# Slot reads of the first two batches at slots 24 and 29, last two loads of x behind them, and block sums of w_out at slots 13 to 20

## The chip, the core and the metric

The kernel runs on one core of a Trainium2 chip. The metric is the device time of one execution in microseconds (us); the median of ten executions stands for the kernel. A separate profiled execution gives the trace from which all durations below come.

## What is computed

An attention step between a sequence and a small set of state slots is followed by a feed-forward layer with a squared ReLU. The reference, cut to what matters:

```python
B, H, S, Ns, D = 8, 8, 512, 32, 64          # x: B,H,S,D   state: B,H,Ns,D
scale = 1 / sqrt(D)
a     = softmax(scale * x @ state.T)         # over the 32 slots
xread = a @ state                            # B,H,512,64
a2    = softmax(scale * state @ x.T)         # over the 512 positions
sread = a2 @ x                               # B,H,32,64: the "slot read"
X   = concat([xread, sread], axis=2) -> (8*544, 512)
h   = X @ w_in                               # 512 -> 2048
g   = s * relu(h)**2 + b
out = g @ w_out                              # 2048 -> 512, float32
```

## The kernel before

**Slots.** The first 128 of 144 slots belong to the eight batches, 16 to each: slot 16*s + f computes hidden block f (128 of 2048 features) of batch s for its 512 sequence rows. The last 16 slots do the same for the 256 rows of all slot reads. `mm1_x` puts the hidden block into PSUM (two matmuls, tile `h`), ACT applies the ReLU, DVE squares it (`g`). Everything else is attached to slots: `at(slot, fn, ...)` puts a function into a table, and the main loop runs, for each slot, first `mm1_x`, then the functions of that slot in the order in which they were entered, then a share of the second layer's matmuls (tile `o`), taken from `units2`.

**The second layer.** Batch 0 is done plainly in 16 units in slots 11 to 28, into two PSUM banks (`ob`), and evacuated by `mm2_out` (tiles `osb`). Batches 1 to 7 use a scheme with seven block products in place of eight: it needs sums of blocks of g (`pair_sums`, tile `pd`, DVE) and sums of blocks of w_out (`weight_sums(q)`, tile `u`, four DVE instructions for each of the four quarters of w_out). Batch 1's part starts at slot 30.

**Attention of a batch b.** `att_T(b)` makes the scores T from the transposed state and the transposed x; ACT takes the exponential E with its sums. `att_D` and `mm1_x` use E for the sequence side. `att_M` folds the state into w_in (tile `M`). For the slot side, `att_aT(b)` scales E (tile `a`, printed by the profile as `a<-E,q`) and transposes it by two DMA transposes on SP's queue into `aT`; `att_V(b)` multiplies it with x (tile `V`, 32 small matmuls), a DVE copy puts it into `sr`, and one more DMA transpose on SP's queue puts it into `srdT`, which is needed only after slot 128.

**x.** `load_x(b)` is a DMA on POOL's queue that converts to 16 bits on the way; `xn` has six buffers, so batch 6 takes batch 0's buffer and has to wait for `att_V(0)`, and batch 7 waits for `att_V(1)`. For batches 3 to 7 x is transposed by four DMA transposes per batch on SP's queue (`dma_xT`, tile `xT`, two buffers); batches 0 to 2 are transposed on TensorE (`xTps`). The state of batches 3 to 7 is transposed by one DMA, `dma_stT` (tile `stTd`, slot 22).

**Order.** PE, POOL and SP run in the order in which the program writes the instructions; DVE's and ACT's order is made by a scheduler. `aT` has two buffers, so `att_aT(2)` has to wait until `att_V(0)` has read `aT` of batch 0. All of it together, around the change:

```python
    at(21, att_aT, 0)
    at(22, dma_stT)
    for k in range(4):
        at(23 + k, dma_xT, 3, k)
    at(27, att_aT, 1)
    ...
    for b in range(B):
        at(NKF * max(b, 2) + (12 if b != 0 else 8), att_V, b)
```

With NKF = 16 the slot reads of batches 0, 1 and 2 stand at slots 40, 44 and 44, that of batch b from 3 on at slot 16*b + 12. A loop sets `att_T(2)` to slot 22, `att_aT(2)` to slot 27, and `att_T(3)` to slot 32; `dma_xT(4, k)` is entered at slots 28 to 34.

Of the kernel before, what the change touches and what calls it, by code (L numbers as in the profile page):

```python
# [14 lines left out]
def kernel(  # L15
# [13 lines left out]
    nc = tc.nc  # L29
    AF = mybir.ActivationFunctionType  # L30
    ALU = mybir.AluOpType
# [5 lines left out]
    P = 128  # L37
    NKM = DM // P
    NKF = DF // P
# [315 lines left out]
    def at(slot, fn, *args):  # L355
        AT.setdefault(slot, []).append(lambda: fn(*args))
# [14 lines left out]
    at(16, att_stT, 2)  # L371
    at(19, att_xT, 2, 0)
    at(20, att_xT, 2, 1)
    at(21, att_aT, 0)
    at(22, dma_stT)
    for k in range(4):
        at(23 + k, dma_xT, 3, k)
    at(27, att_aT, 1)
    units = []
    for b in range(2, B):  # L380
        units += [(att_T, b)] + [(att_M, b, c) for c in range(4)]
# [1 line left out]
    while i < len(units):  # L383
        for u in units[i : i + 2]:
            at(int(slot), *u)
            if u[0] is att_T:
                b = u[1]
# [6 lines left out]
        i += 2  # L394
        slot += 5.2 if i < 6 else 6.4
    for b in range(B):
        at(NKF * max(b, 2) + (12 if b != 0 else 8), att_V, b)


    G = {}  # L400
# [1 line left out]
    hS = S // 2  # L402
# [18 lines left out]
    def blocks(b, j):  # L421
        return G[b, j].rearrange("p (i k) (h t) -> p i (k h) t", k=2, h=2)

    def pair_sums(b, j):

        g4 = blocks(b, j)
        pd = ppool.tile([P, 2, 4, hS], FP16, name=f"pd_{b}_{j}", tag="pd")
        nc.vector.tensor_tensor(  # L428
            pd[:, :, 0:2],
            g4[:, :, 0:4:3, :],  # L430
            g4[:, :, 1:2, :].to_broadcast((P, 2, 2, hS)),
            ALU.subtract,
        )
        nc.vector.tensor_tensor(pd[:, :, 2], pd[:, :, 0], g4[:, :, 3], ALU.add)  # L434
        nc.vector.tensor_tensor(pd[:, :, 3], g4[:, :, 2], pd[:, :, 2], ALU.subtract)  # L435
        PD[b, j] = pd

# [3 lines left out]
    def wo_blk(q, k, h):  # L441
        return wo[q].rearrange("p (i k) (h n) -> p k h i n", k=2, h=2)[:, k, h]

    def weight_sums(q):
        u = upool.tile([P, 4, 2, hD], FP16, name=f"u_{q}", tag="u")
        held = tc.keep_in_program_order
        held(nc.vector.tensor_tensor(u[:, 0], wo_blk(q, 0, 0), wo_blk(q, 0, 1), ALU.subtract))
        held(nc.vector.tensor_tensor(u[:, 1], wo_blk(q, 1, 1), u[:, 0], ALU.subtract))
        held(
            nc.vector.scalar_tensor_tensor(  # L450
                u[:, 2], wo_blk(q, 0, 1), -1.0, wo_blk(q, 1, 1), ALU.mult, ALU.subtract
            )
        )
        held(nc.vector.tensor_tensor(u[:, 3], wo_blk(q, 1, 0), u[:, 1], ALU.subtract))
        U.append(u)

# [198 lines left out]
    att_M(0, 0)  # L655
    warm_up(2)
    for q in range(4):
        at(20 + 3 * q, weight_sums, q)
    at(41, load_x, 6)
    at(45, load_x, 7)  # L660
    for slot in range(NKF * (B + 1)):
        s, f = divmod(slot, NKF)
        if s < B:
            mm1_x(s, f, s == 0 and f in (7, 8))
        else:
            mm1_sr(f)
        for fn in AT.get(slot, []):
            fn()
        run_units(slot)
        if 0 < s < B and f % 4 == 3:  # L670
            pair_sums(s, f // 4)
# [42 lines left out]
```

## Time and profile before

| what | value |
|---|---|
| median of 10 executions | 226.61 us (226.09 to 229.21) |
| profiled execution, its own time | 228.12 us |
| span in the profile | 226.3 us, so 1.8 us lie around it |
| granted TensorE clock, mean over the span | 0.975 |
| TensorE (PE) busy with matmuls | 209.0 us, 92% of the span |
| VectorE (DVE) busy | 167.6 us, 74% |
| ScalarE (ACT) busy | 131.2 us, 58% |
| DMA | 24.04 MB, mean 106 GB/s |

In the profile, PE is TensorE's matmul and PEld its weight load; a line number such as L67 is often that of a helper (all matmuls are issued by `mm` at L67), so tiles tell more than lines. The slice rows of the page cut the span into 40 equal slices of 5.66 us. In a timeline a row gives the start, the length, the instruction, how many were merged, and in brackets how long the engine had been idle before it and for whom. "q0" is the DMA ring set that POOL's DMAs use, "q1" the one that SP's use.

### The profile page before, as it was taken

The page shows a single profiled execution, that of the slowest core. Times are in us where ns is not written, and L with a number is a line of the kernel's source. Part 1 is how long each engine was busy: PE and PEld are TensorE (multiplying, and loading weights), DVE is VectorE, ACT ScalarE, POOL GpSimd, SP SyncE. Part 2 cuts the span into 40 slices and gives each one's busy share as a digit, 9 for nine tenths or more (in the row PEclk, how much of TensorE's full clock was granted, in tenths as well). Part 3 has the DMA queues.
Part 4 walks back from the last instruction along what each step waited for, and adds up shares of the span by engine and source line. Part 5 has one row for each costly group of instructions (what it writes and reads, how often), then busy time and mean ns, then how long its engine had stood idle before and what let it go on. Part 6 is the DMA issues. An engine that isn't in the chain of part 4 may idle for free.

```text
span 226.3 us, 4920 instructions
## 1 busy us (share of the span) xinstructions
PE 209.0 (92%) x1966; PEld 132.0 (58%) x1966; DVE 167.6 (74%) x394; ACT 131.2 (58%) x287; POOL 34.1 (15%) x56
## 2 busy tenths in 40 slices
PE   7978899997999499999999999999999999999970
PEld 2423343543567247667667667666676776888650
DVE  2478836899999627898798879888987888745330
ACT  3486962398786234885785659749855554432200
POOL 5545002201011301102111110120112102100000
PEclk9999999999999959999999999999999999999996
DMA  7999999999211999343354312312312102111211
GB/s 203 194 198 200 178 192 146 180 234 124 86 49 24 176 177 211 84 91 105 93 127 63 101 47 63 82 52 62 81 46 96 49 6 89 59 46 49 93 25 68
DMA packets 41186, 24.04 MB, mean 106 GB/s; under 512 B 25676, under 2 KB 39244, under 8 KB 41164
## 3 DMA queue, kind: packets, MB, share of 16 engines
q0 software_dynamic: 13744, 15.21, 34.0%
q1 hardware_dynamic: 26860, 8.40, 22.7%
q8 instruction: 15, 0.25, 0.5%
q10 hardware_dynamic: 560, 0.13, 0.3%
q14 instruction: 7, 0.06, 0.1%
HBM read 17.37 MB, written 8.91 MB: 116 GB/s over the span
## 4 chain that ended last, share of the span: by engine, by line
PE 63%; DMA 19%; DVE 13%; POOL 2%; issue 0%; ACT 0%
PE o L67 38%; PE h L67 16%; DMA xn<-in_x_dram 10%; DMA stf<-in_state_dram 4%; DMA aT<-a 3%; PE h_sr L67 3%; DVE g L416 3%; PE Mps L67 3%; DVE pd L428 1%; DVE u L450 1%; PE V L67 1%; DMA ident<-ident_const 1%; DVE c L518 1%; DVE pd L435 1%; DVE M L318 1%; PE D L67 1%
## 5 line engine op out<-in xcount | busy, mean ns | idle before, releaser
L415 ACT ACTIVATE g<-h 128x512 f16<-128x512 f32 x126 | 75.2, 604 | 61.6 <-PE h L67 60.7
L67 PE MATMUL h<-a,M 128*128 128x512 f16 x256 | 76.9, 383 | 0.5 <-DVE a L297 0.3
L416 DVE TENSOR_TENSOR g<-g 128x512 f16<-128x512 f16 x128 | 53.6, 423 | 18.3 <-ACT g L415 17.6
L67 PEld LDWEIGHTS <-pd 128*128 128x128 f16 x448 | 43.2, 98 | 17.5 <-issue 2.7
L67 PEld LDWEIGHTS <-g 128*128 128x128 f16 x400 | 38.1, 99 | 23.2 <-issue 6.5
L67 PE MATMUL o<-wo,g 128*128 128x256 f16 (+1 forms) x288 | 46.8, 297 | 1.9 <-DVE osb L471 1.0
L67 PE MATMUL o<-u,pd 128*128 128x256 f16 x336 | 45.9, 273 | 0.0
L528 POOL DMA_DIRECT2D out_dram<-c x24 | 16.2, 675 | 112.9 <-DVE c L523 92.0
L67 PEld LDWEIGHTS <-M 128*128 128x128 f16 x256 | 24.7, 99 | 9.9 <-issue 1.8
L316 ACT CAST M<-Mps 128x512 f16<-128x512 f32 x46 | 24.9, 604 | 0.5 <-PE Mps L67 0.5
L518 DVE SCALAR_TENSOR_TENSOR c<-o,s_bc,bias_bc 128x512 f32<-128x512 f32 x28 | 20.9, 747 | 2.8 <-PE o L67 2.3
L428 DVE TENSOR_TENSOR pd<-g 128x1024 f16<-128x1024 f16 x28 | 19.3, 688 | 0.6
L67 PE MATMUL o<-u,g 128*128 128x256 f16 x112 | 17.2, 291 | 0.0
L523 DVE SCALAR_TENSOR_TENSOR c<-o,s_bc,c 128x512 f32<-128x512 f32 x21 | 15.7, 746 | 1.6 <-PE o L67 1.6
L318 DVE CAST M<-Mps 128x512 f16<-128x512 f32 x18 | 12.3, 685 | 5.2 <-PE Mps L67 5.2
L67 PE MATMUL o<-wo,pd 128*128 128x256 f16 x112 | 15.7, 273 | 0.0
L415 ACT ACTIVATE g_sr<-h_sr 128x256 f16<-128x256 f32 x16 | 6.1, 383 | 12.1 <-PE h_sr L67 12.1
L280 ACT ACTIVATE E<-T 128x256 f16<-128x256 f32 x32 | 11.9, 399 | 2.0 <-PE T L67 2.0
L435 DVE TENSOR_TENSOR pd<-g,pd 128x512 f16<-128x512 f16 x28 | 11.7, 418 | 0.1
L434 DVE TENSOR_TENSOR pd<-pd,g 128x512 f16<-128x512 f16 x28 | 11.7, 418 | 0.1
L293 ACT ACTIVATE D<-D 128x512 f32<-128x512 f32 x16 | 9.7, 610 | 0.0
L295 ACT ACTIVATE R<-D 128x512 f16<-128x512 f32 x16 | 9.5, 600 | 0.3
(63 smaller groups left out, 156.3 us busy)
## 6 DMA issues: line engine op xcount, KB each, us to landing
out_dram<-c POOLq DMA_DIRECT2D x24, 256.0 KB, 2.6
xn<-in_x_dram POOLq DMA_DIRECT2D x7, 512.0 KB, 23.4
wi<-in_moe_w_in_dram POOLq DMA_DIRECT2D x4, 512.0 KB, 12.0
wo<-in_moe_w_out_dram POOLq DMA_DIRECT2D x4, 512.0 KB, 18.5
xf<-in_x_dram SPq DMA_DIRECT2D x4, 256.0 KB, 3.1
out_dram<-osb POOLq DMA_DIRECT2D x4, 256.0 KB, 9.0
out_dram<-c SPq DMA_DIRECT2D x4, 256.0 KB, 2.5
stf<-in_state_dram SPq DMA_DIRECT2D x1, 320.0 KB, 13.1
```

The costliest lines, as they stand in the source:

```text
L67: return nc.tensor.matmul(out, lhsT, rhs, start=start, stop=stop, tile_position=tp, is_transpose=is_transpose, skip_group_check=True,)
L280: nc.scalar.activation(E[:, 256 * m : 256 * m + 256], T[m][:, g, :], AF.Exp, scale=scale, accum_out=rs[:, g, m : m + 1],)
L316: nc.scalar.copy(dst, ps[g])
L318: nc.vector.tensor_copy(dst, ps[g])
L415: nc.scalar.activation(gt, hps, AF.Relu)
L416: nc.vector.tensor_mul(gt, gt, gt)
L428: nc.vector.tensor_tensor(pd[:, :, 0:2], g4[:, :, 0:4:3, :], g4[:, :, 1:2, :].to_broadcast((P, 2, 2, hS)), ALU.subtract,)
L434: nc.vector.tensor_tensor(pd[:, :, 2], pd[:, :, 0], g4[:, :, 3], ALU.add)
L435: nc.vector.tensor_tensor(pd[:, :, 3], g4[:, :, 2], pd[:, :, 2], ALU.subtract)
L518: nc.vector.scalar_tensor_tensor(t, src, s_bc, add, ALU.mult, ALU.add)
L523: nc.vector.scalar_tensor_tensor(t, src, s_bc, t, ALU.mult, ALU.add)
L528: (nc.sync if b == B - 1 else nc.gpsimd).dma_start(dst[:, rows:SCH:2, hD * h : hD * h + hD], t)
```

## The change

The slot reads of batches 0 and 1 move from slots 40 and 44 to slots 24 and 29. `att_aT(0)` moves from slot 21 to 18, `att_aT(1)` from slot 27 to 19, so that on SP's queue the transposes of batch 1's `a` now stand in front of `stTd` and of the transposes of batch 3's x. `load_x(6)` moves from slot 41 to 25 and `load_x(7)` from slot 45 to 30. The four `weight_sums` move from slots 20, 23, 26, 29 to 13, 15, 17, 20, and signs are turned round in them and in `pair_sums`, so that the third instruction of each is a plain add of two blocks in place of a `scalar_tensor_tensor`; `pair_sums` keeps its three instructions.

```diff
@@ order of the slots
     at(19, att_xT, 2, 0)
     at(20, att_xT, 2, 1)
-    at(21, att_aT, 0)
+    at(18, att_aT, 0)
+    at(19, att_aT, 1)
     at(22, dma_stT)
     for k in range(4):
         at(23 + k, dma_xT, 3, k)
-    at(27, att_aT, 1)
...
     for b in range(B):
-        at(NKF * max(b, 2) + (12 if b != 0 else 8), att_V, b)
+        at((24, 29)[b] if b < 2 else NKF * b + 12, att_V, b)
@@ pair_sums
         nc.vector.tensor_tensor(
             pd[:, :, 0:2],
+            g4[:, :, 1:2, :].to_broadcast((P, 2, 2, hS)),
             g4[:, :, 0:4:3, :],
-            g4[:, :, 1:2, :].to_broadcast((P, 2, 2, hS)),
             ALU.subtract,
         )
-        nc.vector.tensor_tensor(pd[:, :, 2], pd[:, :, 0], g4[:, :, 3], ALU.add)
+        nc.vector.tensor_tensor(pd[:, :, 2], g4[:, :, 3], pd[:, :, 0], ALU.subtract)
         nc.vector.tensor_tensor(pd[:, :, 3], g4[:, :, 2], pd[:, :, 2], ALU.subtract)
@@ weight_sums
-        held(nc.vector.tensor_tensor(u[:, 0], wo_blk(q, 0, 0), wo_blk(q, 0, 1), ALU.subtract))
-        held(nc.vector.tensor_tensor(u[:, 1], wo_blk(q, 1, 1), u[:, 0], ALU.subtract))
-        held(
-            nc.vector.scalar_tensor_tensor(
-                u[:, 2], wo_blk(q, 0, 1), -1.0, wo_blk(q, 1, 1), ALU.mult, ALU.subtract
-            )
-        )
+        held(nc.vector.tensor_tensor(u[:, 0], wo_blk(q, 0, 1), wo_blk(q, 0, 0), ALU.subtract))
+        held(nc.vector.tensor_tensor(u[:, 1], wo_blk(q, 1, 1), u[:, 0], ALU.add))
+        held(nc.vector.tensor_tensor(u[:, 2], wo_blk(q, 0, 1), wo_blk(q, 1, 1), ALU.add))
         held(nc.vector.tensor_tensor(u[:, 3], wo_blk(q, 1, 0), u[:, 1], ALU.subtract))
@@ main loop's table
     for q in range(4):
-        at(20 + 3 * q, weight_sums, q)
-    at(41, load_x, 6)
-    at(45, load_x, 7)
+        at((13, 15, 17, 20)[q], weight_sums, q)
+    at(25, load_x, 6)
+    at(30, load_x, 7)
```

## The prediction

> **What bounds the kernel now.** I read the granted clock first, then the busy time by stretches, then PE's timeline where the clock drops, then the waits of SP's queue.
>
> ```profile
> PE   7978899997999499999999999999999999999970
> ...
> PEclk9999999999999959999999999999999999999996
> ```
>
> Each digit is a slice of 5.66 us; counted from 0, PE is busy only 4 tenths of slice 13 (73.5 to 79.2 us), and the granted clock falls in slice 14. By stretches:
>
> ```profile
> 30.00:40.00 10.00, 9.20 (x66) 3.55 (x59) 5.83 (x11) 4.83 (x9) 1.51 (x3) 1.00 1.41 165
> ...
> 50.00:60.00 10.00, 8.52 (x80) 4.05 (x79) 10.00 (x26) 7.33 (x15) 1.08 (x2) 1.00 1.04 138
> 60.00:70.00 10.00, 10.00 (x87) 6.80 (x85) 9.96 (x26) 9.06 (x23) 0.68 (x1) 1.00 0.08 28
> 70.00:80.00 10.00, 6.76 (x136) 4.67 (x135) 7.40 (x19) 2.98 (x5) 3.15 (x4) 0.93 0.91 129
> 80.00:90.00 10.00, 10.00 (x70) 5.88 (x69) 4.83 (x11) 4.55 (x8) 0.67 (x1) 0.73 1.36 194
> ```
>
> The columns after the stretch are its length and the busy time of PE, PEld, DVE, ACT, POOL, then clock, DMA share and GB/s. DVE is full from 50 to 70 us and 4.2 us idle between 30 and 40. PE's timeline names the hole:
>
> ```profile
> 75.56 0.56 PE L67 MATMUL V<-xn,aT 128*32 128x64 f16 x48
> 79.36 0.41 PE L67 MATMUL V<-xn,aT 128*32 128x64 f16 x16 [3.24 <-DMA aT<-a]
> 79.69 1.67 PE L67 MATMUL o<-u,g 128*128 128x256 f16 x7
> ```
>
> The slot reads of batches 1 and 2 stand together at slot 44, and that of batch 2 waits 3.24 us for its transposes. They were issued only at 70.8 and 72.1 us, because:
>
> ```profile
> SPq L329 <- PE V L67: 16.8, 1, 16.8
> ```
>
> SP's queue stood 16.8 us until slot read 0 (slot 40, 70.3 us) had given its `aT` buffer back. After the hole, seven `o` matmuls take 1.67 us in place of 0.77. Behind 85.5 us I see no PE idle time until the tail: the kernel is bound by PE there. Between 33 and 212 us PE waits five times in all: 3.2 us (this one), 1.0 for the eviction of `osb` at 56.0, 0.8 for x of batch 2 at 40.0, 0.3 for g at 59.6, 0.2 for g at 54.5.
>
> **What the Trainium skill says.** "TensorE: Matmul & The Clock Gate", Part 1 (the HAM clock gate): PE's clock is halved after about one idle window of 3.4 us of a free-running counter, and restored after a busy one. The trace agrees: the clock lost (1 - 0.93) * 10 + (1 - 0.73) * 10 = 3.4 us, or 6.8 us at half speed, two windows, from 78.5 to 85.4 us, beginning 2.4 us into the hole. "DMA: Bandwidth & Descriptors", section on queues, rings and completion order: each DMA engine takes turns between the queues packet by packet. The trace agrees; in 42 to 44 us, POOL's and SP's queues moved
>
> ```profile
> q0 software_dynamic: 412, 0.21, 85.6%
> q1 hardware_dynamic: 418, 0.11, 53.2%
> ```
>
> (packets, MB), so a load of x (512 KB in 512 B packets, 1024 of them) takes turns with some 1024 packets of transposes, two `xT` pieces' worth.
>
> **The change, part by part.**
>
> *Slot reads at 24 and 29.* Each is 32 matmuls, 0.35 us of PE before and after: a move, no cost. Slot 24 begins at 47.6 us. Its `aT` is there: at 47.47 us DVE overwrites the source of these transposes without any wait. `aT` of batch 1 now follows directly on SP's queue. The queue's bytes (1.69 MB from stf to the last `aT` of batch 1, ended at 55 us) say that batch 0 is done near 39 us; another 0.26 MB at the 0.058 MB/us of shared stretches is 4.5 us, so 44 to 47 us; slot 29 is at 53.6. I take no wait for either. `aT(2)` no longer waits for slot 40: it is issued near 56 us and read at 75. So the hole goes: **-3.24 us**, and with it the half clock, of whose 3.4 us 0.4 lie in the hole: **-3.0 us**.
>
> *Block sums earlier, plain adds.* A group costs DVE 3 * 0.42 + 0.68 = 1.94 us before and 4 * 0.42 = 1.68 after: 1.04 us less in all. Three groups (5.0 us) go into slots 13 to 17, 28 to 37 us, where DVE has over 4 us free; the first layer's squares and the copies of M there have 1 us or more in hand, and the bias sum comes some 0.4 us later, hidden by PE's 0.8 us wait for x of batch 2. Should that cover be gone, up to 0.5 us. From 46 to 62 us DVE loses 5.8 us of work, so the evictions and squares that PE waited for there come in time: 0.97 + 0.29 + 0.21 = **-1.47 us**. `pair_sums` has the same three instructions of the same shapes (0.69 and 0.42 us): nothing.
>
> *What SP's queue pays.* Its new order is aT(0) x2, aT(1) x2, stTd, xT(3) pieces 0 and 1, srdT(0), pieces 2 and 3, aT(2) x2, xT(4). The pieces of xT(3) are needed by `att_T(3)`, slot 32, 58.87 us before; there they landed by 54.75 us (issued at 48.35, 6.4 us to landing), 4.1 us early. Now (a) 0.26 MB of aT(1) is ahead of them; (b) pieces 2 and 3 stand behind srdT(0), which waits for DVE's copy of slot read 0: after `pd` of batch 1, by the order of the changed program, near 50.7 us, so piece 3 is issued near 53.4 in place of 48.35; (c) the load of x of batch 6, on POOL's queue at slot 25, begins to move near 51 us and takes turns with them for 1024 packets, 4.4 us at 235 packets/us, and the load of batch 7 begins near 57 us. A piece issued under a load of x took 6.4 to 9.6 us to land in this trace (the 9.6 at 77.9 us, under the load of batch 7). So piece 3 lands between 59.8 and 63 us; I take 61.1. Lower bound: 53.4 plus the 2.5 us of an undisturbed transpose, 55.9, no wait. Upper bound: the same mix in 71 to 87 us (two loads of x, 0.78 MB of transposes) took 15.5 us; from 49.5 us this gives 65. `att_T(3)` is reached at 58.87 - 1.2 + 0.7 (two slot reads now ahead of it) = 58.4 us, and its last quarter 0.3 us later. So PE waits 61.1 - 58.7 = **+2.4 us** (0 to 6.3). Behind it in PE's order stands everything.
>
> *The clock in that wait.* A hole of 3.24 us, with 0.9 us of small matmuls inside the same window, was enough before. One of 2.4 us is enough if a window covers most of it; then the wait is nearly over when the clock drops, and one window at half speed costs 3.4 / 2 = 1.7. I take **+1.6 us** (0 to 3.0).
>
> *The loads of x* are read first by the transposes of batch 6 from slot 57 on, 25 slots after the new issue: their own landing is free. The output DMAs behind them on POOL's queue wait for slot reads 0 and 1, now done by then: nothing.
>
> **Sum**: -3.24 - 3.0 - 1.47 + 2.4 + 1.6 = -3.7 us. Against the profiled execution's own 228.12 us this is 224.4; that execution lies 1.5 us above the median of 226.61, and from the median it is 222.9.
>
> **Rivals.**
> 1. *The transposes are hidden anyway.* SP's queue alone moved 0.12 MB in half a microsecond at 54 us; if the load of batch 6 is through before the last pieces and that of batch 7 starts later, they land by 58.7. Against it: three things delay them and only 4.1 us was in hand. Then -7.7: 218.9 us.
> 2. *A wait takes the place of the one removed, and more (slower).* Place: `att_T(3)` at slot 32, for xT(3) pieces 2 and 3; price: their landing less 58.7 us, plus 3.0 for two cold windows. It decides from a landing at 63.4 us (wait 4.7 us), and is slower by over 0.5% from 64.5. For it: between 74 and 76 us the transposes moved 26 packets beside 643 of a load. With 65 us: wait 6.3, sum +1.6, 228.2 us.
> 3. *DVE was no bound and the moved sums hurt.* Then the 1.47 stays and 0.5 is added: 224.9 us with the forecast's wait.
> 4. *The change doesn't remove the hole*: aT(2) is late again, since it stands behind srdT(0) and xT(3) on one queue. It has 19 us; 226 us or more. Unlikely.
>
> **How the numbers follow.** No change can be told within 0.5% (1.1 us). The forecast's mechanism, a wait of 1 to 4.5 us: 0.56 (0.45 faster; 0.11 within 1.1 us, a long wait with two cold windows). Rival 1: 0.16, faster. Rival 2: 0.16 (0.14 slower, 0.02 within). Rival 3: 0.08, half faster, half within. Rival 4, and waits on the crowded DMA engines before 60 us that I don't see: 0.04, of which 0.03 slower and 0.01 within. Faster: 0.45 + 0.16 + 0.04 = 0.65; within: 0.11 + 0.02 + 0.04 + 0.01 = 0.18; slower: 0.14 + 0.03 = 0.17. The range, 219.0 to 227.4, runs from rival 1 to the beginning of rival 2; the likeliest case alone is 221 to 225.5.
>
> **What would show it.** Right: no PE wait for aT after 70 us, the clock row without the low digit in slice 14, `u` adds of 0.42 us before 46 us, and a PE wait of 1 to 4 us for DMA xT before the T matmuls of batch 3 near 58 us. Rival 1 shows no such wait; rival 2 one over 4.7 us with two slices of low clock. Wrong altogether: a wait at slot 24 or 29 for aT, or DVE still full from 50 to 60 us.

## The result, and the profile after

The changed kernel takes 228.84 us (median of 15 executions), the kernel before 226.75 us (median of 50): ratio 1.0095, 95% interval 1.0073 to 1.0118, about 2.1 us slower. The forecast was 222.9 us and faster. The profiled execution has a time of its own of 229.08 us and a span of 227.2 us. The runs below come from several chips, so every ratio is to the kernel before on the same chip, where its median lay between 226.75 and 227.86 us. An execution more than 1.5% above the fastest of its kernel counts as slow and is left out of the ratios and intervals, while a median is over all executions.

The same two rows of the page:

```profile
PE   7989999899469999999999999999999999999970
...
PEclk9999999999959999999999999999999999999995
```

Counted from 0, slice 13 is full now, and the hole is in slices 10 and 11 (56.8 to 68.2 us); the low clock moved from slice 14 to slice 11. By stretches (length, busy PE, PEld, DVE, ACT, POOL, then clock, DMA share, GB/s):

```profile
50.00:60.00 10.00, 9.36 (x106) 4.44 (x105) 9.13 (x23) 8.04 (x17) 2.91 (x4) 1.00 1.62 173
60.00:70.00 10.00, 5.50 (x30) 3.03 (x30) 2.72 (x8) 2.96 (x11) 0.00 (x0) 0.66 1.52 192
70.00:80.00 10.00, 10.00 (x88) 6.91 (x86) 9.04 (x20) 7.76 (x15) 0.68 (x1) 1.00 0.54 118
80.00:90.00 10.00, 10.00 (x115) 6.63 (x113) 7.84 (x17) 5.64 (x10) 2.03 (x3) 1.00 0.25 84
```

Everything that the change was to remove is gone: PE is full and the clock is whole from 70 to 90 us, and DVE is no longer full from 50 to 60. In its place there is one stretch in which every engine is idle while the DMA engines are busy. PE's timeline says what it waits for:

```profile
59.01 0.39 PE L67 MATMUL T<-xT,stTd 64*32 64x256 f16 x8
63.82 0.61 PE L67 MATMUL T<-xT,stTd 64*32 64x256 f16 x4 [4.42 <-DMA xT<-xn]
65.11 0.60 PE L67 MATMUL T<-xT,stTd 64*32 64x256 f16 x4 [0.68 <-DMA xT<-xn]
65.65 1.68 PE L67 MATMUL o<-wo,g 128*128 128x256 f16 x7
```

The T matmuls of batch 3 do the two pieces of x that are there (x8), then wait 4.42 us for piece 2 and 0.68 us for piece 3. The seven `o` matmuls behind them take 1.68 us, the half clock. This is the place that the prediction named for its wait, and for its second rival. SP's queue and POOL's queue at the time:

```profile
45.51 2.51 SPq L226 DMA_TRANSPOSE xT<-xn  x2
51.35 1.13 SPq L349 DMA_TRANSPOSE srdT<-sr  x1
52.52 3.15 SPq L226 DMA_TRANSPOSE xT<-xn  x2
```

```profile
50.18 0.91 POOL L146 DMA_DIRECT2D xn<-in_x_dram  x1 [8.20 <-ACT D L293]
54.02 0.55 POOL L468 DMA_DIRECT2D out_dram<-osb  x1 [2.92 <-DVE osb L467]
56.55 0.54 POOL L468 DMA_DIRECT2D out_dram<-osb  x1 [1.97 <-DVE osb L467]
57.08 0.91 POOL L146 DMA_DIRECT2D xn<-in_x_dram  x1
```

Pieces 2 and 3 are issued at 52.5 and 53.9 us, behind the transpose of slot read 0, as forecast (53.4). The loads of batches 6 and 7 are issued at 50.2 and 57.1. The landing is not as forecast: piece 3 was put at 61.1 us, and the matmul that needs it starts at 65.1. Nor does the load of batch 6 move when it was thought to, from 51 to some 55.4 us. Its packets are of 512 B, those of a transpose of 256 B, so the packets of a stretch that are "under 2 KB" but not "under 512 B" are those of loads of x. From 53 to 55 us and from 55 to 61 us:

```profile
DMA packets 519, 0.26 MB, mean 131 GB/s; under 512 B 461, under 2 KB 487, under 8 KB 518
DMA packets 1874, 1.08 MB, mean 180 GB/s; under 512 B 778, under 2 KB 1779, under 8 KB 1874
```

These are 26 packets of 512 B in the first stretch and 1001 in the second, nearly the 1024 of one load: the load of batch 6 ran after 55 us, on top of pieces 2 and 3. The two queues between 54.5 and 57.5 us (packets, MB, share of 16 engines):

```profile
q0 software_dynamic: 324, 0.22, 146.1%
q1 hardware_dynamic: 162, 0.04, 14.5%
```

At the 235 packets per us and queue of the prediction, 700 packets of SP's queue would have gone in these 3 us. 162 went.

### The profile page after: what moved, and what is told of

It reads as the page before. It is cut to its first block, busy times and chain, and to the rows that moved or that the text cites. A ratio compares the mean times of both kernels' runs of the same rounds, so it can differ in the third digit from the quotient of the medians.

```text
span 227.2 us, 4919 instructions
## 1 busy us (share of the span) xinstructions
PE 209.8 (92%) x1966; PEld 132.8 (58%) x1966; DVE 168.3 (74%) x394; ACT 131.3 (58%) x287; POOL 34.5 (15%) x56
## 4 chain that ended last, share of the span: by engine, by line
PE 70%; DMA 21%; DVE 2%; POOL 2%; ACT 1%; SPq 1%; issue 0%
PE o L67 43%; PE h L67 19%; DMA xn<-in_x_dram 11%; DMA xT<-xn 5%; DMA stf<-in_state_dram 4%; PE h_sr L67 3%; PE Mps L67 3%; DMA ident<-ident_const 1%; PE D L67 1%; PE V L67 1%; PE T L67 1%; POOL wi L156 1%; ACT E L280 1%; POOL wo L166 1%; SPq L226 1%; DVE g L416 1%
## 5 line engine op out<-in xcount | busy, mean ns | idle before, releaser
L415 ACT ACTIVATE g<-h 128x512 f16<-128x512 f32 x126 | 75.6, 606 | 55.8 <-PE h L67 54.8
L67 PE MATMUL o<-wo,g 128*128 128x256 f16 (+1 forms) x288 | 47.7, 301 | 0.4 <-DMA wo<-in_moe_w_out_dram 0.4
L67 PE MATMUL o<-u,g 128*128 128x256 f16 x112 | 15.7, 273 | 0.0
L434 DVE TENSOR_TENSOR pd<-g,pd 128x512 f16<-128x512 f16 x28 | 11.7, 418 | 0.2
L435 DVE TENSOR_TENSOR pd<-g,pd 128x512 f16<-128x512 f16 x28 | 11.7, 418 | 0.2
L67 PE MATMUL warm_ps<-warm 128*128 128x512 f16 x22 | 9.1, 549 | 1.5 <-DVE warm L83 1.2
L67 PEld LDWEIGHTS <-stTd 64*32 64x32 f16 x240 | 2.9, 90 | 12.3 <-issue 12.1
```

The source lines that it names most:

```text
L67: return nc.tensor.matmul(out, lhsT, rhs, start=start, stop=stop, tile_position=tp, is_transpose=is_transpose, skip_group_check=True,)
L415: nc.scalar.activation(gt, hps, AF.Relu)
L434: nc.vector.tensor_tensor(pd[:, :, 2], g4[:, :, 3], pd[:, :, 0], ALU.subtract)
```

## The experiments

Theory A says that the early loads of x, taking turns with the transposes, made the wait; theory B says that the new order on SP's queue made it.

**Both loads late** (`e1_loads_late`, and again on another chip as `r2_loads_late`):

```diff
-    at(25, load_x, 6)
-    at(30, load_x, 7)
+    at(41, load_x, 6)
+    at(45, load_x, 7)
```

> The changed kernel with the loads of x of batches 6 and 7 back at slots 41 and 45; all else as changed. Theory A (the loads take turns with the transposes on the DMA engines, and that made the 5.1 us wait of the T matmuls of batch 3): that wait falls to under 1 us, the half clock near 62 to 69 us is gone, about 8 us less: 220 to 221 us. Theory B (the new order on SP's queue made it: the transposes of batch 1's a and of slot read 0 in front): the wait stays above 3 us with the half clock, 226 to 229 us.

> The changed kernel with both loads back at slots 41 and 45 again, on the same chip as the others of this call: the same ratio as the first time, 0.965 to 0.98, and no wait for xT.

Measured: 221.53 us, ratio 0.9721 (0.9645 to 0.9797); again 221.46 us, 0.9714 (0.9665 to 0.9764). PE's timeline of the first, and its two queues between 54.5 and 57.5 us:

```profile
58.77 0.57 PE L67 MATMUL T<-xT,stTd 64*32 64x256 f16 x16
```

```profile
q1 hardware_dynamic: 797, 0.19, 92.7%
q0 software_dynamic: 101, 0.33, 30.7%
```

All sixteen T matmuls run in one go, with no wait. With the same order on SP's queue and pieces 2 and 3 issued from 52.3 us on, the transposes moved 797 packets where the changed kernel moved 162. Without the early loads, then, the new order does no harm.

**The transposes of batch 1's a behind batch 3's x** (`e2_aT1_behind`):

```diff
     at(18, att_aT, 0)
-    at(19, att_aT, 1)
     at(22, dma_stT)
     for k in range(4):
         at(23 + k, dma_xT, 3, k)
+    at(27, att_aT, 1)
...
-        at((24, 29)[b] if b < 2 else NKF * b + 12, att_V, b)
+        at((24, 34)[b] if b < 2 else NKF * b + 12, att_V, b)
...
-    at(30, load_x, 7)
+    at(35, load_x, 7)
```

> The changed kernel with the transposes of batch 1's a back behind those of batch 3's x (slot 27), so slot read 1 goes to slot 34 and the load of batch 7 to slot 35. Theory A: the load of batch 6 still runs beside the last two pieces; the wait of the T matmuls stays at 3 to 5 us, 226 to 229 us. Theory B: 0.26 MB less in front of the pieces lets them land 2 to 4.5 us earlier; the wait falls to 0.5 to 3 us, 221 to 225 us.

Measured: 223.49 us, ratio 0.9782 (0.9711 to 0.9852).

```profile
61.04 0.85 PE L67 MATMUL T<-xT,stTd 64*32 64x256 f16 x8 [1.47 <-DMA xT<-xn]
```

The wait fell to 1.5 us, as theory B said, with the load of batch 6 still at slot 25. Here the load of batch 7 and slot read 1 moved too; `e8_load7_late` below shows what the later load of batch 7 is worth alone.

**The transpose of slot read 0 behind batch 3's x** (`e3_srd_behind`):

```diff
-        nc.sync.dma_start_transpose(srdT[:, b].rearrange("p k j -> p (k j)"), sr)
+        def give():
+            nc.sync.dma_start_transpose(srdT[:, b].rearrange("p k j -> p (k j)"), sr)
+        if b == 0:
+            at(27, give)
+        else:
+            give()
```

> The changed kernel with the transpose of slot read 0 moved out from between the pieces of batch 3's x on SP's queue, to behind them. The last two pieces are then issued right after the first two, near 48 to 50 us and not at 52.5 and 53.9. Theory A: they still run beside the load of batch 6 and land at 60 us or later; the wait falls by 1 to 3 us, 225 to 228 us. Theory B: they land before 59 us, no wait, 220 to 221 us.

Measured: 226.27 us, ratio 0.9816 (0.9712 to 0.992). The four executions lie between 223.2 and 228.6 us, and only two enter the ratio, so the time says little here and the profile has to decide. The four pieces are now issued in one go from 44.6 to 49.9 us; 0.2 and 2.5 us of the wait remain:

```profile
58.65 0.39 PE L67 MATMUL T<-xT,stTd 64*32 64x256 f16 x4 [0.23 <-DMA xT<-xn]
61.50 0.61 PE L67 MATMUL T<-xT,stTd 64*32 64x256 f16 x4 [2.46 <-DMA xT<-xn]
```

That is theory A's size, 2.4 us less than in the changed kernel: issued over 4 us earlier, the last piece still has the load beside it.

**The load of batch 6 alone early** (`e8_load7_late`): `at(30, load_x, 7)` becomes `at(45, load_x, 7)`.

> The changed kernel with only the load of batch 7 back at slot 45; the load of batch 6 stays at slot 25. The run without either early load had no wait for xT. If the load of batch 6 alone makes the wait (its 1024 packets run from 51 to 56 us, beside the pieces): 3 us or more stay, 226 us or more. If the load of batch 7, which begins near 57 us, holds up the last pieces: the wait falls under 2 us, 221 to 224 us.

Measured: 228.44 us, ratio 1.0025 (0.9999 to 1.0052). Its profiled execution is one of its longer ones (229.99 us); in it the wait is 4.4 us:

```profile
62.62 0.39 PE L67 MATMUL T<-xT,stTd 64*32 64x256 f16 x4 [2.66 <-DMA xT<-xn]
64.72 0.61 PE L67 MATMUL T<-xT,stTd 64*32 64x256 f16 x4 [1.71 <-DMA xT<-xn]
```

The load of batch 7 is worth some 0.7%; the load of batch 6 alone keeps the kernel 3% above the one with both loads late. Most of the fall to 1.5 us in `e2_aT1_behind` is then due to the order on SP's queue, not to the later load of batch 7.

**The early load with the old order** (`e11_old_order_load6`): the edits of `e2_aT1_behind` and `e3_srd_behind` together, with the load of batch 7 at slot 45 and that of batch 6 still at slot 25.

> The changed kernel with the load of batch 6 still at slot 25, but with the old order on SP's queue: the four pieces of batch 3's x right behind stTd, then the transposes of batch 1's a (slot 27), with the transpose of slot read 0 behind them; slot read 1 at 34, the load of batch 7 at 45. If the early load hurts whatever the order is: the wait for xT stays over 1.5 us, 223.5 us or more. If it takes both, the load beside the pieces and the pieces pushed back: no wait for xT, ratio 0.97 to 0.98, as with the loads late.

Measured: 221.35 us, ratio 0.973 (0.9672 to 0.9787), and no wait for xT:

```profile
57.52 0.40 PE L67 MATMUL T<-xT,stTd 64*32 64x256 f16 x16
```

So neither theory is right alone. The early load of batch 6 makes no wait for xT when the pieces stand in front of it in time, and the new order makes none when no load runs beside it. It takes both. A smaller wait appears here, 0.8 us of a slot read for aT at 61 us.

**Both loads just behind the T matmuls** (`e10_loads_behind_T3`): slots 33 and 37.

> The changed kernel with the loads of batches 6 and 7 at slots 33 and 37, just behind the T matmuls of batch 3, and not at 25 and 30. Theory A: all that counts is that they don't run beside the pieces of batch 3's x; no wait for xT, as with the loads at 41 and 45: ratio to before about 0.97. Theory B: any early load hurts somewhere else (the transposes of batch 4's x, needed at slot 51): a wait for xT or aT of over 1 us between 65 and 90 us.

Measured: 222.21 us, ratio 0.9747 (0.9698 to 0.9796), no PE wait above 0.4 us behind the 0.7 us for x of batch 2 at 41 us. An early load is no evil by itself: between slot 25 and slot 33 the wait goes.

**The wait filled with work** (`e4_warm`):

```diff
+        if b == 3:
+            warm_up(21)
         T = [att_ps([P, NG, S // 2], FP32, f"T_{b}_{m}") for m in range(2)]
```

> The changed kernel with 21 matmuls of 128x512 on a tile that nobody reads, set in front of the T matmuls of batch 3 on PE (4.5 us of PE). It separates the wait from the clock. If the half clock after the wait is the cost of PE standing idle, the wait is filled, the clock stays at 1.00 and about 3 us are saved: 225 to 226.5 us. If the clock falls for another reason, the time stays at 228 to 229.5 us.

Measured: 228.21 us, ratio 1.0016 (0.9987 to 1.0045), against 1.0095 and 1.0100 for the changed kernel itself, measured on other chips: 0.8%, 1.9 us less and not the expected 3. In the profiled execution:

```profile
63.07 0.79 PE L67 MATMUL T<-xT,stTd 64*32 64x256 f16 x16
```

```profile
60.00:70.00 10.00, 10.00 (x78) 5.99 (x77) 4.88 (x12) 5.60 (x16) 0.68 (x1) 1.00 1.41 184
```

The clock is 1.00 behind the T matmuls, so the half clock is a cost of PE's idleness. The median itself falls into the range that was set for the other case, and it is the clock that decides. This execution is the fastest of the twenty (225.82 us), and in it the T matmuls end 1.9 us earlier than in the profile of the changed kernel, so the pieces had landed sooner too: it can't price the clock. The ratios can, roughly, at 1.9 us. In the profile of the changed kernel, the stretch behind the T matmuls has a clock of 0.67, so (1 - 0.67) * 4.35 = 1.4 us were lost there:

```profile
65.65:70.00 4.35, 4.35 (x24) 2.77 (x23) 2.12 (x6) 2.51 (x10) 0.00 (x0) 0.67 1.78 170
```

**The hole of the kernel before, filled** (`e9_before_filled`):

```diff
+        if b == 2:
+            warm_up(14)
         ps = att_ps([P, NG, D], FP32, f"V_{b}")
```

> The kernel before with 14 matmuls of 128x512 on a tile that nobody reads (3.0 us of PE) in front of slot read 2, so that PE works through its hole near 76 us. It prices the half clock of the kernel before. If every execution pays it, as the forecast took it: about 3 us less. If only a part of the executions pays it, as the granted clocks of the runs say (a mean of 3.9 to 4.3 us of clock lost, against 2.1 in kernels without a hole): 1.5 to 2 us less, and the lost clock falls to 2 us in all of them.

Measured: 226.42 us, ratio 0.9958 (0.9931 to 0.9985): 1.0 us less (0.3 to 1.6), not 3 and not 1.5 to 2. In the profiled execution the slot read follows the filling without a wait:

```profile
77.12 3.19 PE L67 MATMUL warm_ps<-warm 128*128 128x512 f16 x14
80.24 0.50 PE L67 MATMUL V<-xn,aT 128*32 128x64 f16 x32
```

Every execution comes with its mean granted clock; (1 - clock) * span is the clock time lost. It is 1.8 us on average in this kernel, 3.4 us in the kernel before on the same chip (30 executions, from 1.1 to 5.7), and 5.7 and 5.9 us in the changed kernel (34 executions on two chips, 31 of them above 5). The profiled execution of the kernel before, with (1 - 0.975) * 226.3 = 5.7 us, was one of its dearest in this respect. The 1.0 us is a lower bound for the price of the clock: over all 40 executions the kernel before lost 3.9 us, and the medians are 1.4 us apart; and where the hole is shorter than the filling's 3.1 us (it is 2.4 in the profile of `e6_sums_only` below), the filling itself delays slot read 2.

**The changed kernel again** (`r1_after_again`), no edit:

> The changed kernel as it is, on the chip of the next three, to have all on one chip and to see how the wait of the T matmuls of batch 3 varies from one execution to the next. Theory A and B alike: that wait is 4 to 6 us with the half clock behind it, about 1% slower than before.

Measured: 229.71 us, ratio 1.0100 (1.0069 to 1.0132); the waits of the T matmuls were 3.69 and 0.86 us in its profiled execution, whose own time, 228.12 us, is 1.6 below the median.

**Slot reads alone, without what they cost** (`e5_reads_only`): the kernel before with reads 0 and 1 at slots 33 and 37.

```diff
-        at(NKF * max(b, 2) + (12 if b != 0 else 8), att_V, b)
+        at((33, 37)[b] if b < 2 else NKF * b + 12, att_V, b)
```

> The kernel before with slot reads 0 and 1 at slots 33 and 37, just behind the T matmuls of batch 3; the loads of x stay at 41 and 45, the transposes of batch 1's a stay behind those of batch 3's x, and the block sums stay as they were. It has the gain of the reads without what SP's queue and the DMA engines paid. If the forecast's first terms hold (hole 3.24, half clock 3.0): about 220.5 us, no wait for aT, none for xT. If the hole only moves on to another wait, 224 us or more.

Measured: 224.78 us, ratio 0.9864 (0.9805 to 0.9924), 3.1 us less (1.7 to 4.4), half of what the first two terms say. The hole is gone; PE's waits from 45 to 210 us are these:

```profile
PE o L67 <- DVE osb L471: 1.0, 1, 1.0
PE Mps L67 <- DVE sr L347: 0.7, 1, 0.7
PE o L67 <- DVE g L416: 0.3, 1, 0.3
PE h L67 <- ACT g L415: 0.2, 1, 0.2
```

The first, third and fourth were there before, and one new wait of 0.7 us is for DVE's copy of a slot read. This alone doesn't make up what is missing of the 6.2 us; the price of the clock in `e9_before_filled` says where most of the rest lies.

**Block sums alone** (`e6_sums_only`), the edits of `weight_sums`, `pair_sums` and their slots in the kernel before:

> The kernel before with the block sums alone as in the changed kernel (slots 13, 15, 17, 20, plain adds, signs turned round). If the forecast's third term holds: the PE waits for osb, g and g between 54 and 60 us are gone, the hole near 76 us stays, 1.5 us less: about 225.2 us. If DVE was no bound there: no change, or up to 0.5 us more.

Measured: 225.9 us, ratio 0.9975 (0.9939 to 1.0011). The interval holds no gain, and it ends just short of the 0.65% that was expected (a ratio of 0.9935). In the profile the waits of the `o` matmuls for `osb` and for g are gone, one of 0.2 us for g stays, and the hole stays, at 2.4 us. In this execution the granted clock is 1.00 from 20 us to the tail: that hole cost no clock.

**Reads and sums together** (`e7_reads_and_sums`), the edits of the last two:

> The last two together: slot reads at 33 and 37 and the block sums of the changed kernel; loads of x and SP's order as before. If the terms add up: 226.7 - 7.7 = about 219 us, with no PE wait above 0.5 us between 45 and 210 us. If they don't: near the reads alone.

Measured: 223.06 us, ratio 0.9787 (0.9704 to 0.987). The waits from 45 to 210 us are down to one:

```profile
PE h L67 <- ACT g L415: 0.2, 1, 0.2
```

The waits go as forecast; the time, 4.8 us less (3.0 to 6.7), falls short of the 7.7.

## Why the prediction was wrong

- **The hole at slot 44 (-3.24 us)**: right. It is gone, no slot read waits for its aT at slot 24, 29 or 44, and slot read 2's transposes are issued at 55.8 us (forecast 56).
- **The half clock behind it (-3.0 us)**: mis-sized. The term was read from one execution, in which the hole cost two windows of half clock. Filling the hole brings 1.0 us, 1.4 by the medians over all executions: many executions don't lose that much clock there. The gains of the change without its cost are 2.8 to 2.9% in the two runs with late loads, 6.4 us in place of 7.7, though the wider of the two intervals (4.6 to 8.1 us) holds both.
- **Block sums (-1.47 us)**: the waits went, as the profiles show; the gain alone stays unclear (0.9939 to 1.0011). The later bias sum was hidden or nearly so: one profile (`r1_after_again`) has a PE wait of 0.24 us for it.
- **The wait of the T matmuls (+2.4 us)**: this step failed. The place, the new order and the issue times of the pieces were right. The landing was not: 65.1 us in place of 61.1, so 5.1 us of waiting, 2.7 more. Two parts of its working were off. It had the load of batch 6 moving from 51 us on, and so through by some 55.4; the load moved from 55 to 61 us. And it let the two queues take equal turns at 235 packets per us, with 6.4 to 9.6 us from issue to landing; pieces 2 and 3 took over 11 us, because for 3 us, when the load of batch 6 was starting, SP's queue moved 162 packets. The trace before had shown such a stretch, 26 packets against 643 between 74 and 76 us; the prediction quoted it for its rival and did not put it into its own sum. Its upper bound, timed on a whole stretch of 71 to 87 us, gave 65 us, and that is what came, in part by luck: SP's queue moved 0.92 MB in that stretch, not 0.78, and 0.64 MB from 49.5 to 65.1 us after the change.
- **The half clock behind the wait (+1.6 us)**: about right, 1.9 us by the filled run and 1.4 in the profile. But here nearly all executions pay it, where the kernel before pays its own only in part.

With these sizes, gains of 6.4, wait 5.1 and clock 1.9, the sum is +0.6 us against 2.1 measured. The ratios put the whole cost at 3.8%, 8.7 us. Part of the gap is a term that the prediction left out: broken into three goes, the T matmuls themselves take 0.39 + 0.61 + 0.60 = 1.6 us in place of 0.57 in `e1_loads_late`. Profile against profile, the first layer's matmuls of slot 28 start at 53.48 us and those of slot 36 at 71.85 in the changed kernel, at 53.23 and 64.07 in `e1_loads_late`: these eight slots cost 7.5 us more. The 1.2 us from there to 8.7 are less than the interval of `e1_loads_late` (1.7 us to each side), and the wait differs from execution to execution (5.1 and 4.6 us in two profiled ones), so these runs don't settle them.

The second rival was the right case, with 228.2 us; it had a chance of 0.16. That it met the measured 228.84 so closely is partly luck too, since its sum holds the gains of 7.7. Rival 1's 218.9 us, 3.4% less than before, is the kernel that the loads at 41 and 45 make; it measured 2.8 to 2.9% less.

## What to carry to other kernels

A bulk load that is only wanted much later is not free because its own landing is: ask which transfers with a due time run beside it, and put it behind the consumer of those (here slot 33 in place of 25: 2.5% faster than before instead of 1% slower), or put those transfers in front of it in time (`e11_old_order_load6`: 2.7% faster). When an earlier stretch of the same trace shows a like mix of transfers, time that stretch as a whole beside the sum built from fair turns; here the whole stretch came nearer, in one case. A clock penalty read from one profiled execution is one draw: look at the granted clock of all executions before it goes into a sum.

## What the runs showed of the hardware

Two things were not expected. When a load on POOL's queue starts, transposes on SP's queue can all but stand still for 2 to 3 us (26 packets against 643 in the kernel before, 162 against 324 after the change, 114 against 602 from 55 to 58 us in `e8_load7_late`) instead of taking equal turns, as they do in the middle of a load (412 against 418 in the kernel before). It doesn't always happen: in `e11_old_order_load6` the same load begins at 54 us, and from 54 to 56 us the queues moved 451 packets against 470. What makes the difference was not tried. And the kernel with a PE hole of about 3.2 us in its profile loses from 1.1 to 5.7 us of clock in all, execution by execution, while the one with a wait of about 5 us loses over 5 us in 31 of 34; 1.8 us of this are lost with the hole filled too. How long the hole was in the executions that were not profiled isn't known.
